# Softmax scores and the first mixture's front product on eight 64x32 tiles of TensorE, with a new load order

## The chip, the cores and the metric

One core of a Trainium2 chip runs the whole program. The metric is the device time of one execution in microseconds, the median of several runs. The profile is taken on one further execution of the same program.

## What is computed

Four batches of eight heads, 576 tokens, 64 numbers a head. 32 packed rows `p` attend to `k` and `v`; the tokens `q` then attend to the 32 packed results. What comes out (2304 tokens of 512 numbers) goes through a layer with `h * cos(h)` and through a mixture of four experts. All is float32; the weights of the first layer arrive as float64.

```
p_packed = softmax(p k^T / 8) v              # 32 rows a head
attn     = softmax(q p_packed^T / 8) p_packed
h = attn @ w_in ; g = h * cos(h) ; x = g @ w_out      # 512 -> 2048 -> 512
out = sum over e of p[:, e] * (relu(x @ w1[e]) @ w2[e])   # 512 -> 1024 -> 512
```

## The kernel before

The program has three parts that flow into each other.

**Attention.** A unit is four of the 32 (batch, head) pairs, so there are eight units; units 2b and 2b+1 make batch b. `attn_p` makes a unit's scores of the packed rows (line `f_s1`, L339), the row maxima (L344), the exponentials (L354), their transposes (L360, copied by L364), the product with `v` (L375), and from it, scaled and masked, the transposed packed rows `ptf` (L380, L386, L390). `attn_q` makes the scores of the tokens (L419), transposes them on VectorE (L425) and does the softmax: maxima, subtraction on GpSimd (L434), exponential (L438), sums, multiplication on GpSimd (L450), transposition (L454), and a split into a rounded part and a remainder (L459, L463), together called `at`. The products L339 and L419 are in plain float32; each holds two heads in 128 rows, with zeros where the heads would mix, and gives 64 columns, so that two of them fill the array.

**First layer, "MoE1".** The 2048 hidden columns go in four groups G of 512. The first product is folded: `m_front` (L508) multiplies the packed rows by `w_in`, once for each G and batch, 16 times in all; `a_front` multiplies the result by `at` (three products each, L193 to L195, for rounded part and remainder), and does the cosine; `a_back` multiplies by `w_out`. `w_block` decodes float64 weights into float32: Abs and a scaling on ScalarE (L249, L270), clamp, shift and sign on VectorE (L256, L260, L265), an addition on GpSimd (L278), and for `w_out` also the split (L274 on ScalarE, L281 on GpSimd). Blocks of `w_in` in group 0 are decoded in halves.

**Second layer, "MoE2".** `b_pair` and `b_back`, the last two thirds of the time, which the change doesn't edit.

The order of the instructions on each engine is fixed when the program is built. Each step is an operation of a planner (`Plan`) with an engine, a duration, the operations that it needs and the buffers that it takes; `Plan.run` goes through time and picks on each engine the ready operation with the lowest key. TensorE and the loads have keys from a table written by hand (`KEYS`). An operation with `alt` may go from GpSimd to VectorE. Loads all stand in one queue, SP's. The raw float64 blocks share two buffers (`raw64`), so the third block waits until GpSimd has finished with the first. Where TensorE has a planned gap in the first 31 us, products of the identity (L966) fill it.

Of the kernel before, what the change touches and what calls it, by code (L numbers as in the profile page):

```python
# [25 lines left out]
class Plan:  # L26
# [32 lines left out]
    def run(self):  # L59
# [14 lines left out]
        while done < len(self.ops):  # L74
# [3 lines left out]
            for eng, l in todo.items():  # L78
                cand = []
                for o in l + ([o for o in todo["POOL"] if o["alt"]] if eng == "DVE" else []):  # L80
                    t = max(o["at"], free.get(eng, 0.0), port if o["port"] else 0.0)
                    ok = True
                    if eng == "PE" and o["key"] > pe[0][0] + self.AHEAD:
                        ok = False
                    for s in o["take"]:
                        if not ends[s["tag"]] or self.bufs[s["tag"]] > 0 and s["no"] != taken[s["tag"]]:
                            ok = False
                            break
                        t = max(t, min(ends[s["tag"]]) + 0.07)
                    if ok:  # L90
                        cand.append((t, o))
                if not cand:
                    continue
                t0 = min(t for t, _ in cand)

                cost = lambda o: 8 * (o["table"] not in (None, table)) if eng == "ACT" else 15 * (o["eng"] != eng)
                t, _, _, o = min((t, o["key"] + cost(o), o["n"], o)
                                 for t, o in [(max(t, t0), o) for t, o in cand if t <= t0 + 0.05])
                if best is None or (t, o["n"]) < best[:2]:
                    best = (t, o["n"], o, eng)  # L100
# [34 lines left out]
def tile_packed_attention_moe_moe2(ctx: ExitStack, tc: tile.TileContext, qT, kT, vk, pT, w_in, w_out, dp, w1, w2, out):  # L135
# [71 lines left out]
    mask = cst.tile([P, P], F32, name="mask")  # L207
    nc.vector.memset(mask, 0.0)
    for i in range(4):
        nc.vector.memset(mask[32 * i:32 * i + 32, 64 * (i % 2):64 * (i % 2) + 64], 1.0)  # L210

    pl = Plan({"pa": -4, "t": -5, "g": 8, "m": 2, "at": 2, "raw64": 2, "wd": 4, "T": 2, "w": 4, "yh": 8, "pz": -2,
               "raw": 4, "s": 4, "aop": 8, "w2": 8, "ys": 5, "pt": -6, "g2": 13, "oacc": NTT,
               **{"B" + x: 1 for x in ("b11", "t1", "t2", "t3", "t4", "b21", "b22")}})
    MB = 1 / 0.27

    def dma(us, f, after=(), take=(), use=(), key=None):
        return pl.op("SP", us, f, after, take, use, key)
# [6 lines left out]
    def w_block(what, G, k, key, pieces=1, ld_key=None):  # L225
# [7 lines left out]
        def f_load():  # L233
            s["raw"] = t = dec.tile([P, 2, 512, 2], U32, tag="raw64", name="raw64", bufs=2)
            load(t.rearrange("p c a b -> p c (a b)"), rows(src.bitcast(U32), r0, slice(2 * c0, 2 * (c0 + cn))))

        ld = dma(1.05 * MB, f_load, take=[sraw], key=key if ld_key is None else ld_key)
        s["ready"] = []
        head = G < HEAD_G
        for p in range(pieces):  # L240
# [31 lines left out]
            def f_hi(c=c):  # L272
                s["w"] = wo.tile([P, 2, 2, 512], F32R, tag="w", name="w", bufs=4)
                nc.scalar.activation(s["w"][:, :, 0], s["D"].bitcast(F32), AF.Copy)  # L274
# [5 lines left out]
            def f_lo(c=c):  # L280
                nc.gpsimd.tensor_tensor(out=s["w"][:, :, 1], in0=s["D"].bitcast(F32), in1=s["w"][:, :, 0].bitcast(F32),  # L281
                                        op=ALU.subtract)


            a = pl.op(*("ACT", 1.15 * r) if head else ("DVE", 0.72 * r), f_and, [ld], [sd] if p == 0 else [], [sraw, sd],
                      key, port=not head)
            a = pl.op("DVE", 0.72 * r, f_clamp, [a], [], [sd], key, port=True)
# [4 lines left out]
            h = pl.op("ACT", 1.1, f_hi, [a], [sw], [sd], key) if what == "out" else None  # L292
            a = pl.op("POOL", 2.45 * r, f_add, [a, l, h], [], [sraw, sd], key)
            if what == "out":
                a = pl.op("POOL", 2.45, f_lo, [a], [], [sw, sd], key)
# [5 lines left out]
    pbd = cst.tile([P, 2, 4, 2, 64], F32, name="pbd")  # L301
    un, ptfs, ats, at_d = {}, {}, {}, {}
    ld_p = dma(2.5 + 0.52 * MB, lambda: load(pbd, pT), key=-2000)

    def load_kv(n, vtag, key):
# [11 lines left out]
        s["ld_v"] = dma(0.59 * MB, f_v, take=[s["v"]], key=key + 0.1)  # L317
# [10 lines left out]
    def attn_p(n, keys):  # L328

        s = un[n]  # L330
        pb = pbd[:, n // 4, n % 4]
        p1, p2, p3, p4 = (pl.slot("pa") for _ in range(4))
        ta, tT, tz = pl.slot("t"), pl.slot("T"), pl.slot("pz")
# [8 lines left out]
        def f_mx():  # L342
            s["mx"] = mx = small.tile([P, 1], F32, tag="mx", name="mx")
            nc.vector.tensor_reduce(out=mx, in_=s["s1"][:, :, :S2], op=ALU.max, axis=AX.XY)  # L344

        def f_nb():
            mx = s["mx"]
            s["nb"] = nb = small.tile([P, 1], F32, tag="nb", name="nb")
            nc.vector.tensor_scalar(out=nb, in0=mx, scalar1=-SCALE, scalar2=None, op0=ALU.mult)
# [679 lines left out]
```

## Time and profile before

| | |
|---|---|
| runs | 1169.66 us median of 3 (1167.9 to 1172.15) |
| profiled execution | span 1170.3 us from first to last instruction; no time outside the span is listed |
| TensorE busy in the span | 1138.4 us (97%) |
| VectorE, ScalarE, GpSimd busy | 752.7, 526.3, 410.2 us |
| mean granted clock of TensorE | 0.991 |

TensorE's share is that of the whole span. The table says nothing about when the other 32 us lie, or which work of the 1138.4 us the change touches; the views by stretch and by line do.

### The profile page before, as it was taken

How to read it: one execution, taken by the hardware profiler on the slowest of the kernel's cores; microseconds unless marked ns; L12 is line 12 of the kernel's file. 1: busy time of each engine (PE TensorE's matmuls, PEld its weight loads, DVE VectorE, ACT ScalarE, POOL GpSimd, SP SyncE). 2: the span in 40 equal slices, each digit the busy share in tenths (PEclk: the TensorE clock that was granted, in tenths of full speed). 3: DMA queues.
4: the chain of work that ended last, by engine and by line, in shares of the span. 5: the costliest groups of instructions: out<-in, count | busy, mean ns of one | idle time of the engine just before them, and what ended most of it. 6: DMA issues, size and time to landing. Idle time of an engine off the chain costs nothing.

```text
span 1170.3 us, 17323 instructions
## 1 busy us (share of the span) xinstructions
PE 1138.4 (97%) x6816; PEld 1023.6 (87%) x6816; DVE 752.7 (64%) x1179; ACT 526.3 (45%) x889; POOL 410.2 (35%) x286
## 2 busy tenths in 40 slices
PE   6599999999999999999999999999999999999998
PEld 5468889989899988998998899989988999899897
DVE  4686867744445777666667666666666666666653
ACT  3778866655555653333334433333335433333320
POOL 1665754443222554122223722222224522222210
PEclk9799999999999999999999999999999999999999
DMA  9854442411215433122224332222231412222101
GB/s 285 285 188 163 169 150 96 153 42 41 82 41 173 134 113 108 58 69 55 72 73 126 108 90 73 72 73 73 72 108 46 136 57 70 55 71 73 54 1 54
DMA packets 54160, 115.96 MB, mean 99 GB/s; under 512 B 5824, under 2 KB 18112, under 8 KB 52032
## 3 DMA queue, kind: packets, MB, share of 16 engines
q1 hardware_dynamic: 54080, 114.87, 30.4%
q8 instruction: 53, 0.87, 0.3%
q14 instruction: 27, 0.22, 0.1%
HBM read 100.70 MB, written 14.16 MB: 98 GB/s over the span
## 4 chain that ended last, share of the span: by engine, by line
PE 91%; DVE 3%; DMA 3%; ACT 2%; POOL 1%; issue 1%; SPq 0%; DVEq 0%; ACTq 0%
PE pa L193 29%; PE pa L195 29%; PE pa L194 29%; PE pa L508 3%; DMA kt<-kT 3%; PE pa L339 1%; PE pa L419 0%; POOL w L628 0%; DVE bop L628 0%; DVE dt L265 0%; PE pa L375 0%; ACT t L539 0%; DVE dt L256 0%; DVE t L542 0%; POOL dt L278 0%
## 5 line engine op out<-in xcount | busy, mean ns | idle before, releaser
L193 PE MATMUL pa<-bop,aop 128*128 128x384 f32 x672 | 226.5, 337 | 3.4 <-DVE p L771 1.4
L194 PE MATMUL pa<-bop,aop 128*128 128x384 f32 x672 | 225.7, 336 | 0.0
L195 PE MATMUL pa<-bop,aop 128*128 128x384 f32 x672 | 225.6, 336 | 0.0
L193 PE MATMUL pa<-w,g 128*128 128x512 f32 x576 | 224.9, 390 | 0.0
L194 PE MATMUL pa<-w,g 128*128 128x512 f32 x576 | 224.7, 390 | 0.0
L195 PE MATMUL pa<-w,g 128*128 128x512 f32 x576 | 224.7, 390 | 0.0
L840 DVE SCALAR_TENSOR_TENSOR oacc<-pa,pr,oacc 128x512 f32<-128x512 f32 x126 | 94.2, 750 | 137.1 <-PE pa L195 137.1
L628 POOL TENSOR_TENSOR aop<-s,aop 128x512 fp32r<-128x512 f32 x33 | 44.8, 1357 | 352.1 <-ACT aop L637 352.1
L193 PE MATMUL pa<-g,w 128*128 128x288 f32 x512 | 153.0, 299 | 0.1
L194 PE MATMUL pa<-g,w 128*128 128x288 f32 x512 | 151.4, 296 | 0.0
L195 PE MATMUL pa<-g,w 128*128 128x288 f32 x512 | 150.9, 295 | 0.0
L559 POOL TENSOR_TENSOR g<-t,g 128x576 fp32r<-128x576 f32 x64 | 93.7, 1478 | 150.5 <-ACT g L556 143.7
L193 PEld LDWEIGHTS pa<-bop,aop 128*128 128x128 f32 x672 | 126.1, 188 | 12.8 <-DVE g L783 3.5
L628 POOL TENSOR_TENSOR w<-raw,w 128x512 fp32r<-128x512 f32 x91 | 120.3, 1343 | 40.6 <-ACT w L637 33.1
L194 PEld LDWEIGHTS pa<-bop,aop 128*128 128x128 f32 x672 | 126.1, 188 | 4.4
L195 PEld LDWEIGHTS pa<-w,g 128*128 128x128 f32 x576 | 108.1, 188 | 23.3
L195 PEld LDWEIGHTS pa<-bop,aop 128*128 128x128 f32 x672 | 126.1, 188 | 0.0
L194 PEld LDWEIGHTS pa<-w,g 128*128 128x128 f32 x576 | 108.2, 188 | 17.8
L193 PEld LDWEIGHTS pa<-w,g 128*128 128x128 f32 x576 | 108.1, 188 | 17.8
L780 ACT ACTIVATE g<-pa 128x384 fp32r<-128x384 f32 x144 | 70.6, 491 | 114.5 <-DVE pa L771 111.5
L780 ACT ACTIVATE g<-p 128x384 fp32r<-128x384 f32 x48 | 25.2, 525 | 172.0 <-DVE p L771 172.0
L193 PEld LDWEIGHTS pa<-g,w 128*128 128x128 f32 x512 | 96.5, 188 | 5.1 <-issue 4.6
(105 smaller groups left out, 2010.7 us busy)
## 6 DMA issues: line engine op xcount, KB each, us to landing
raw<-w SPq DMA_DIRECT2D x96, 512.0 KB, 3.7
at<-at SPq DMA_DIRECT2D x16, 1152.0 KB, 5.2
raw<-w_in SPq DMA_DIRECT2D x8, 1024.0 KB, 6.5
raw<-w_out SPq DMA_DIRECT2D x8, 1024.0 KB, 5.0
kt<-kT SPq DMA_DIRECT2D x8, 576.0 KB, 6.6
vt<-vk SPq DMA_DIRECT2D x8, 576.0 KB, 9.3
qt<-qT SPq DMA_DIRECT2D x8, 576.0 KB, 11.0
y<-yacc SPq DMA_DIRECT2D x24, 192.0 KB, 2.2
```

The lines of the kernel that those rows point to most:

```text
L193: nc.tensor.matmul(o, lhsT=l(0), rhs=r(0), start=first, stop=False, skip_group_check=True)
L194: nc.tensor.matmul(o, lhsT=l(0), rhs=r(1), start=False, stop=False, skip_group_check=True)
L195: nc.tensor.matmul(o, lhsT=l(1), rhs=r(0), start=False, stop=last, skip_group_check=True)
L339: nc.tensor.matmul(s1[64 * a:64 * a + 64, c, :S2], lhsT=pb[:, a, :], rhs=s["kt"][:, a, c * S2:(c + 1) * S2], start=True, stop=True)
L508: nc.tensor.matmul(o[64 * a:64 * a + 64, g], lhsT=ptfs[2 * bb + g][:, 64 * a:64 * a + 64], rhs=w[g]["D"].bitcast(F32)[:, a ^ (bb % 2)], st ...
L559: nc.gpsimd.tensor_tensor(out=s["g"][:, 1], in0=s["t"], in1=s["g"][:, 0].bitcast(F32), op=ALU.subtract)
L628: (nc.vector if on_vector else nc.gpsimd).tensor_tensor(out=dst[:, 1], in0=src, in1=dst[:, 0].bitcast(F32), op=ALU.subtract)
L780: nc.scalar.activation(g["t"][:, 0], s[src], AF.Relu)
L840: nc.vector.scalar_tensor_tensor(out=oa["t"], in0=ot, scalar=sc, in1=oa["t"], op0=ALU.mult, op1=ALU.add)
```

## The change

The two score products and `m_front` now hold one head in 64 rows and give 32 columns: eight such tiles fill the array, two halves of the rows (e) by four quarters of the columns (q). The packed rows lose their zeros (`ptile` for `pbd`, half the bytes), and the mask is gone. A batch is now one unit: its two score products are one step each, with two results, one for each e, and the softmax behind them runs once for each e as it ran for each unit; one transpose L426 and one copy L430 serve a batch. `w_out` of group 0 is decoded in halves as well, and every load of a block in halves is two loads. Subtraction, multiplication and remainder of the token softmax may go to VectorE. The small load of expert shares and its four VectorE steps (`probs`) move from the start to planned time 60. Loads and steps of the first part have keys of their own, one for each batch.

```diff
+    def half_heads(o, l, r, N):
+        for q, e in HQ:            # (0,0) (0,1) (1,0) ... (3,1)
+            nc.tensor.matmul(o(e)[32 * q:32 * q + 32, :N], lhsT=l[64 * e:64 * e + 64, 32 * q:32 * q + 32],
+                             rhs=r(q // 2, q % 2)[64 * e:64 * e + 64], start=True, stop=True)
...
         def f_s1():
-            s["s1"] = s1 = psum2()
-            for a in range(2):
-                for c in range(2):
-                    nc.tensor.matmul(s1[64 * a:64 * a + 64, c, :S2], lhsT=pb[:, a, :],
-                                     rhs=s["kt"][:, a, c * S2:(c + 1) * S2], start=True, stop=True)
+            s["s1"] = [psum2(), psum2()]
+            for c in range(2):
+                half_heads(lambda e: s["s1"][e][:, c], ptile[:, bb].rearrange("p q r -> p (q r)"),
+                           lambda g, a: u[g]["kt"][:, a, c * S2:(c + 1) * S2], S2)
...
+                half_heads(lambda e: s["s2"][e][:, c], ptfs[bb], lambda g, a: u[g]["qt"][:, a, c * S2:(c + 1) * S2], S2)
...
         def f_mm():
             s["o"] = o = psum2()
-            for g in range(2):
-                for a in range(2):
-                    nc.tensor.matmul(o[64 * a:64 * a + 64, g], lhsT=ptfs[2 * bb + g][:, 64 * a:64 * a + 64],
-                                     rhs=w[g]["D"].bitcast(F32)[:, a ^ (bb % 2)], start=True, stop=True)
+            half_heads(lambda e: o[:, e], ptfs[bb], lambda g, a: w[g]["D"].bitcast(F32)[:, a], 512)
...
+            a = pl.op("POOL", 1.16, f_sub, [a], [], [tx], alt=0.78)
...
+            a = pl.op("POOL", 1.16, f_mul, [a], [], [tx], alt=0.78)
...
+            a = pl.op("POOL", 1.42, f_lo, [a], [], [ta, so], alt=0.78)
...
-    w_block("out", 0, 0, KEYS["out0"], ld_key=-400), w_block("out", 0, 1, KEYS["out0"] + 10, ld_key=-390)
+    w_block("out", 0, 0, KEYS["out0"][0], 2, KEYS["load"]["out"])
+    w_block("out", 0, 1, KEYS["out0"][1], 2, KEYS["load"]["out"] + 1)
...
-    probs()
...
+    plan.append((PROBS, len(plan), probs))
```

What this does to the order is seen at three places. In SP's queue, the loads behind the first four, before (`kt`, `vt`, `qt` are the keys, values and tokens of a unit, `raw64` a block of float64 weights):

```order
L185 DMA raw64_214<-w_in 128x2x1024
L185 DMA raw64_266<-w_in 128x2x1024
L185 DMA kt_288<-kT 128x1152
L185 DMA vt_311<-vk 96x1536
L185 DMA kt_324<-kT 128x1152
L185 DMA vt_336<-vk 96x1536
L185 DMA qt_343<-qT 128x1152
L185 DMA qt_356<-qT 128x1152
L185 DMA raw64_367<-w_out 128x2x1024
L185 DMA raw64_408<-w_out 128x2x1024
```

The same place in the changed kernel:

```order
L190 DMA raw64_185<-w_in 128x1024 x2
L190 DMA raw64_255<-w_in 128x1024 x2
L190 DMA kt_291<-kT 128x1152
L190 DMA kt_302<-kT 128x1152
L190 DMA qt_314<-qT 128x1152
L190 DMA raw64_324<-w_out 128x1024 x2
L190 DMA qt_335<-qT 128x1152
L190 DMA raw64_372<-w_out 128x1024 x2
L190 DMA vt_391<-vk 96x1536
```

Both keys of the second batch now come first, the two values behind the two blocks of `w_out`.

On VectorE, where the second block of `w_in` is finished, before (L344 is the maximum over the scores of a unit, L265 the last VectorE step of a half block):

```order
L344 TENSOR_REDUCE mx<-pa 128x1
L260 TENSOR_SCALAR wd<-wd 128x512
L256 TENSOR_SCALAR wd<-wd 128x512
L265 SCALAR_TENSOR_TENSOR wd<-raw_266,wd 128x512
L260 TENSOR_SCALAR wd<-wd 128x512
L442 TENSOR_REDUCE z_352<-x 128x18
L344 TENSOR_REDUCE mx<-pa 128x1
L265 SCALAR_TENSOR_TENSOR wd<-raw_266,wd 128x512
L349 TENSOR_SCALAR nb<-mx 128x1 x2
```

The same place in the changed kernel (L274 is the old L265, L371 the old L344, L483, L467 and L656 are the multiplication, subtraction and remainder that stood on GpSimd):

```order
L274 SCALAR_TENSOR_TENSOR wd<-raw_255,wd 128x512
L483 TENSOR_TENSOR x<-x,z_322 128x576
L488 STREAM_TRANSPOSE xt<-x 128x576
L467 TENSOR_TENSOR x<-x,m_316 128x576
L656 TENSOR_TENSOR at<-xt,at 128x576
L265 TENSOR_SCALAR dt<-dt 128x512
L475 TENSOR_REDUCE z_376<-x 128x18
L269 TENSOR_SCALAR dt<-dt 128x512
L479 TENSOR_SCALAR z_376<-z_376 128x18
L480 RECIPROCAL z_376<-z_376 128x18
L544 TENSOR_TENSOR m<-pa,m 128x2x512
L371 TENSOR_REDUCE mx<-pa 128x1
```

The maxima of the second batch, which need its keys, now stand behind the last step of the block, no longer ahead of it.

On TensorE, from the scores of the second batch to the first `a_front`, before (L339 scores, L508 the front product, L360 and L375 transposes and product with `v`, L193 the first product of `a_front`):

```order
L966 MATMUL pa<-ident 128x128 x12
L339 MATMUL pa<-kt,pbd 64x288 x8
L508 MATMUL pa<-wd,ptf 64x512 x4
L360 MATMUL pa<-ident,a 96x128 x12
L375 MATMUL pa<-vt,aT 32x64 x48
L386 MATMUL pa<-ident,pz 128x128
L193 MATMUL pa<-at,m 128x288
```

The same place in the changed kernel (L347 is `half_heads`, L386 the transposes, L198 the first product of `a_front`):

```order
L347 MATMUL pa<-qt,ptf 32x288 x16
L347 MATMUL pa<-wd,ptf 32x512 x8
L347 MATMUL pa<-kt,ptile 32x288 x16
L386 MATMUL pa<-ident,a 96x128 x6
L198 MATMUL pa<-at,m 128x288
```

The front product now stands ahead of the second batch's scores, and the products with `v` behind the first `a_front`; the filling products are gone here.

## Rows read from the trace of the kernel before

**Rows 1.** The page: TensorE's busy tenths and granted clock in 40 equal slices.

```profile
PE   6599999999999999999999999999999999999998
...
PEclk9799999999999999999999999999999999999999
```

**Rows 2.** Stretches: ends, length, busy us by engine, PEclk, DMA share, GB/s.

```profile
0.00:64.40 64.40, 42.66 (x420) 29.87 (x420) 34.86 (x74) 33.90 (x53) 29.10 (x24) 0.87 0.91 291
64.40:150.00 85.60, 83.40 (x744) 71.19 (x744) 68.37 (x114) 67.46 (x98) 55.74 (x37) 0.98 0.46 161
150.00:414.90 264.90, 264.90 (x1912) 248.27 (x1909) 159.06 (x202) 154.66 (x226) 107.08 (x65) 1.00 0.31 103
414.90:1170.30 755.40, 747.45 (x3746) 674.26 (x3744) 490.45 (x791) 270.32 (x513) 218.31 (x161) 1.00 0.24 74
```

The engines stand in the order TensorE, its weight loads, VectorE, ScalarE, GpSimd.

**Rows 3.** Groups by shape: count, busy us, mean ns, idle before.

```profile
L508 PE MATMUL pa<-wd,ptf 128*64 128x512 f32 x128 | 34.1, 638 | 0.8 <-POOL wd L278 0.8
L339 PE MATMUL pa<-kt,pbd 128*64 128x288 f32 x64 | 10.6, 453 | 10.2 <-DMA kt<-kT 10.2
```

**Rows 4.** The chain that ended last: front products, start and length.

```profile
60.04 3.41 PE pa L508 x8
...
100.99 1.72 PE pa L508 x8
...
361.91 1.87 PE pa L508 x8
```

**Rows 5.** Timeline of TensorE around one front product, and its line's view.

```profile
149.35 0.29 PE L195 MATMUL pa<-g,w 128*128 128x288 f32 x1
149.57 1.94 PE L508 MATMUL pa<-wd,ptf 128*64 128x512 f32 x8
...
151.68 0.29 PE L194 MATMUL pa<-at,m 128*128 128x288 f32 x1
...
L508 PE MATMUL pa<-wd,ptf x8: 592/592/643, 149.6 to 150.9; 128*64 128x512 f32 x8
```

**Rows 6.** Timeline of TensorE around the scores of one unit.

```profile
97.31 0.29 PE L194 MATMUL pa<-g,w 128*128 128x288 f32 x1
97.44 0.29 PE L195 MATMUL pa<-g,w 128*128 128x288 f32 x1
97.67 1.20 PE L339 MATMUL pa<-kt,pbd 128*64 128x288 f32 x8
...
99.03 0.29 PE L194 MATMUL pa<-g,w 128*128 128x288 f32 x1
```

**Rows 7.** Timeline of TensorE: the product with `v`, 32 columns each.

```profile
106.89 0.88 PE L375 MATMUL pa<-vt,aT 96*32 96x64 f32 x48 [0.29 <-ACT aT L364]
107.70 0.33 PE L386 MATMUL pa<-ident,pz 128*128 128x128 f32 x1
```

**Rows 8.** Timeline of several engines on the way to the first `a_front`.

```profile
33.41 2.20 PE L339 MATMUL pa<-kt,pbd 128*64 128x288 f32 x8 [4.76 <-DMA kt<-kT]
...
35.65 0.76 DVE L344 TENSOR_REDUCE mx<-pa 128x1 f32<-128x576 f32 x1 [3.52 <-PE pa L339]
...
36.32 0.68 DVE L265 SCALAR_TENSOR_TENSOR wd<-raw,wd 128x512 uint32<-128x512 uint32 x1
...
37.15 1.29 POOL L278 TENSOR_TENSOR wd<-raw,wd 128x512 uint32<-128x512 uint32 x1 [4.54 <-DVE nb L349]
...
38.49 1.07 PE L508 MATMUL pa<-wd,ptf 128*64 128x512 f32 x2 [0.84 <-POOL wd L278]
...
43.53 0.38 PE L193 MATMUL pa<-at,m 128*128 128x288 f32 x1
```

**Rows 9.** Two stretches of the head, columns as in rows 2.

```profile
30.00:40.00 10.00, 5.74 (x21) 2.41 (x22) 5.60 (x14) 2.58 (x6) 4.20 (x4) 0.69 0.77 242
40.00:64.40 24.40, 16.67 (x180) 11.68 (x177) 15.94 (x26) 21.14 (x30) 19.22 (x11) 0.79 0.92 321
```

**Rows 10.** ScalarE's groups before 64.4 us: Abs of half and whole blocks.

```profile
L249 ACT ACTIVATE wd<-raw 128x512 f32<-128x512 f32 x4 | 2.7, 670 | 0.7 <-DMA raw<-w_in 0.7
L249 ACT ACTIVATE dt<-raw 128x1024 f32<-128x1024 f32 x2 | 2.3, 1168 | 0.0
```

More of the change, by code (lines that the diff above doesn't have):

```diff
@@ L77, in run @@
                 pe.pop(0)
[L78 to L86, printed above, removed]
-                            ok = False
[L88 to L100, printed above, removed]
@@ new lines, in run @@
+            for ahead in (self.AHEAD, 1e9):
+                if best is not None:
+                    break
+                for eng, l in todo.items():
+                    cand = []
+                    for o in l + ([o for o in todo["POOL"] if o["alt"]] if eng == "DVE" else []):
+                        t = max(o["at"], free.get(eng, 0.0), port if o["port"] else 0.0)
+                        ok = True
+                        if eng == "PE" and o["key"] > pe[0][0] + ahead:
+                            ok = False
+                        need = {}
+                        for s in o["take"]:
+                            k = need[s["tag"]] = need.get(s["tag"], 0) + 1
+                            if len(ends[s["tag"]]) < k or self.bufs[s["tag"]] > 0 and s["no"] != taken[s["tag"]] + k - 1:
+                                ok = False
+                                break
+                            t = max(t, sorted(ends[s["tag"]])[k - 1] + 0.07)
+                        if ok:
+                            cand.append((t, o))
+                    if not cand:
+                        continue
+                    t0 = min(t for t, _ in cand)
+                    cost = lambda o: 8 * (o["table"] not in (None, table)) if eng == "ACT" else 15 * (o["eng"] != eng)
+                    t, _, _, o = min((t, o["key"] + cost(o), o["n"], o)
+                                     for t, o in [(max(t, t0), o) for t, o in cand if t <= t0 + 0.05])
+                    if best is None or (t, o["n"]) < best[:2]:
+                        best = (t, o["n"], o, eng)
@@ L231, in w_block, with f_load @@
         wblk[what, G, k] = s
[L233 to L237, printed above, removed]
+        def f_load(p=0):
+            if p == 0:
+                s["raw"] = dec.tile([P, 2, 512, 2], U32, tag="raw64", name="raw64", bufs=2)
+            t, n = s["raw"], 2 // pieces
+            load(t[:, p * n:(p + 1) * n].rearrange("p c a b -> p c (a b)"),
+                 rows(src.bitcast(U32), r0 + p * P, slice(2 * c0, 2 * (c0 + cn)), n))
+        key_l = key if ld_key is None else ld_key
+        lds = []
+        for p in range(pieces):
+            lds.append(dma(1.05 * MB / pieces, lambda p=p: f_load(p), take=[] if p else [sraw], use=[sraw] if p else [],
+                           key=key_l, begun=lds[-1:]))
         s["ready"] = []
         head = G < HEAD_G
+        prev, his = [], []
         for p in range(pieces):
```

370 lines of the change are left out of this document (202 added, 168 removed), and 3 rows, old and new, of the table KEYS.

## The prediction

> **What bounds the kernel now.** I read the page's slices first. TensorE is busy nine tenths or more in all of the 40 slices but the first two and the last, and its clock falls only in the first ones [rows 1]. So time can come from two places: less work on TensorE where it never stops, or an earlier end of the head, where it waits. The stretches cut the span at three points: the first `a_back` product (64.4 us), the end of the attention work (150) and the first product of MoE2 (414.9). From 150 to 414.9 TensorE is busy 264.90 of 264.90 us while VectorE and ScalarE work under 61% of it: every microsecond taken from TensorE there is a microsecond of the kernel. From 64.4 to 150 it is still busy 83.40 of 85.60, but VectorE (68.37) and ScalarE (67.46) work 80% and 79%. Before 64.4 it is busy 42.66, filling products included, at a mean clock of 0.87 of 2.4 GHz, and the DMA engines are 91% busy. The last stretch holds 747.45 busy of 755.40 and nothing that the change edits [rows 2]. The groups by shape size the work that changes: 128 instructions L508, and 64 L339 that waited 10.2 us for keys [rows 3].
>
> **The front product, 16 times.** Between the ordinary products at 149.35 and 151.68 lie 2.33 us; two of them at their spacing of 0.13 leave 2.06 for the front product. Its eight instructions (four float32 products of two passes each) take 592 ns at the median, 4.7 us together inside 1.94: they overlap by twos, in four rounds whose first and last start 1.3 us apart, so 0.43 a round [rows 5]. That is two cycles a column at the full clock (512 x 2 / 2.4 GHz). Four rounds are 1.71, the rest, 0.35, is the change of tile shape and the run-out. The new product has 16 instructions for eight tiles. If all eight run at once, that is two rounds: 0.86 less. For eight more starts I allow 0.06, under half of what the product with `v` spends on eight of its 48 instructions, everything included (0.81 us from 106.89 to 107.70, 17 ns each) [rows 7]. So **2.06 becomes 1.26: 0.80 less** (bounds 0.72 and 0.86 while the tiles overlap). The trace shows four tiles side by side: 48 instructions of 64 columns in 0.81 are twelve rounds of 0.053 and 0.17 around them [rows 7]. No row shows two halves of the rows at once. The opposite bound is therefore that e = 0 and e = 1 take turns, a rival below.
>
> A rule speaks against the change. The row first: 24 products with `v` of two passes each would need 24 x 0.053 = 1.28 us if the second pass of one held back the first pass of the next tile; they take 0.81 [rows 7]. The Trainium skill (TensorE: Matmul & The Clock Gate, Part 3, on what overlaps) says that matmuls start and end strictly in program order. Were the two passes of each product neighbours in that order, eight tiles would be a staircase of 8 x 0.43 + 0.35 = 3.8 us instead of 1.26. The trace disagrees with that reading for four tiles, and I take the row.
>
> **The scores, four and four.** By the same reckoning one unit's L339 costs 1.59 us from 97.44 to 99.03 less two spacings of 0.13, 1.33, again four rounds, of 0.24 for 288 columns [rows 6]. A batch has 32 instructions in four rounds of eight, so it costs what one unit cost, plus 0.10 for starts: 1.43 instead of 2.66, **1.23 less** (bounds 0.9 and 1.33). L419 has the same shape. One transpose of the packed result for two saves 0.3 a batch [rows 7].
>
> **Where this counts.** (a) 150 to 414.9: eleven front products, 21.2 us apart from 149.6 to 361.91 [rows 4, 5], **8.8 us**, all of it on the path, since no other engine is near its limit. (b) 64.4 to 150: three front products (2.4), scores of batches 2 and 3 (four steps, 4.9) and two transposes (0.6): 7.9. Taking all of it would leave 77.7 us for VectorE's 68.4 and ScalarE's 67.5, 88% and 87%, in chains that go back and forth between engines. TensorE already idles 2.2 us there at 80%. Bounds 0 and 7.9; I take half, **4 us**. The two front products before 64.4 count to the head.
>
> **The head.** Today the last half block of `w_in` is late because of order. The scores of the fourth unit wait for keys until 33.41, the maximum L344 stands ahead of the sign step L265 on VectorE and waits 3.52 us with it, GpSimd waits 4.54 for that, and the front product ends at 39.56, the first `a_front` starts at 43.53 [rows 8]. In the new order the sign step stands ahead of the maximum, so up to 3.5 us go. The keys come ahead of values and tokens, so the second batch's scores find them. But the second batch's first six transposes now stand ahead of the first `a_front`. With the front product done at 39.56 - 3.5 = 36 they follow scores (1.43) and a maximum for each half (0.76 [rows 8]), then an exponential and the transposes themselves, about as long again each: some 40 at the earliest, and VectorE has the remainder of the front product and three new steps to do in between. Of the 3.5 us I give the first `a_front` 1. Between there and the first `a_back` ScalarE bounds: 21.14 busy of 24.40 from 40 us on, while from 30 to 40 it had 2.58 of 10 [rows 9]. With both `w_out` blocks ahead of the second batch's values, and half as many bytes of packed rows, some of its 4.7 us of decoding (two Abs and two scalings of 1.17) moves into that idle time; halves cost it 0.67 twice for 1.17 once, four pairs of Abs and scaling, 0.7 us, and about as much more for the rounded part [rows 10]. Net **2 us** for the head (bounds -2 and +5). Cover for the rest: the subtraction, multiplication and remainder that go to VectorE use the 4.4 us that it idles from 30 to 40 [rows 9]; if that cover is gone they cost 0.8 us each, three times, the duration of the nearest VectorE step of that width, L344. `probs` moves from an idle VectorE into the head's end: four steps under 0.3 us each. Its load stands behind a `w_in` block that waits for GpSimd to free a raw buffer; if it lands late, VectorE waits, and two steps of the cosine queue behind. At 291 GB/s [rows 2] a block of 1.05 MB is 3.6 us, the price of one such collision. No fillers stand between 24 us and the first `a_front`, so those products may run at the lower clock of 1.2 GHz; today the clock is 0.69 and 0.79 of full there too [rows 9], so I take no difference, within the bounds.
>
> **The sum.** 8.8 + 4 + 2 = 14.8 us from the profiled 1170.3: 1155.5. MoE2 keeps its 755.4. The profiled span lies 0.6 above the median of the runs, 1169.66, so the forecast for the median is **1155 us**.
>
> **Rivals.**
> 1. *The other engines take all of the second stretch.* For: both at 80% there. Against: they keep TensorE at 97% now. Then (b) is 0, and if `probs` collides as well the head gains nothing: 1169.7 - 8.8 = 1161, to 1164 with the collision.
> 2. *The head opens up.* If ScalarE's decoding moves fully into the idle time, the head gives 5 and (b) 7: 1169.7 - 8.8 - 12 = 1149.
> 3. *The tiles bring nothing:* four rounds as before, because only the column quarters overlap and the hardware sorts them well. Then the two score steps of a batch and the front product cost what they did and only the head is left: 1168.
> 4. *Slower: the two row halves take turns in the written order.* A column's e = 1 starts when its e = 0 has run both passes (0.86 us), and the next column's e = 0 with it: five turns, 5 x 0.86 + 0.35 = 4.6 us a front product, 2.6 more than now. Fourteen on the path cost 36 us, the four score steps 5.2 for 2.66 each, 10 us: about 1213. It decides from about 2.1 us a front product on. For it: no row shows row halves side by side. Against: weights, moving rows and results of the halves lie on different partitions or in different banks (`o[:, 0]`, `o[:, 1]`), and columns show no such wait [rows 7]. The Trainium skill (same page, Part 3, measured speedups) gives 10.6 times for sixteen tiles over rows and columns, which agrees with 1.26; no run here shows it yet.
>
> **How the numbers follow.** The forecast and its neighbourhood, 1150 to 1160.5, get 0.60, rival 1 0.17, rival 2 0.13, rival 3 0.04, rival 4 0.06. From 1149 to 1164 lie the forecast, most of rival 1 and half of rival 2: about 0.81. A measurement of this kernel can tell about 0.3%, 3.5 us, from no change. Faster by more than that: forecast, rivals 1 and 2, 0.89; within it, rival 3 and a little of rival 1, 0.05; slower 0.06.
>
> **What would show it.** Front products: 16 instructions that all start within half a microsecond, about 1.25 us between ordinary products. First `a_back` near 62 us, first MoE2 product near 400, MoE2 again 755 long. Stretch (b) should show TensorE idle of about 6 us in place of 2.2, with ScalarE or VectorE named as what ended it. I am wrong if front products keep 2 us or more, or if the first `a_back` comes after 66.

## The result, and the profile after

The changed kernel takes 1156.07 us at the median of 4 runs (1154.18 to 1159.73), the kernel before 1169.98 in the same set (4 runs, 1167.9 to 1172.15): a ratio of 0.9886, 95% interval 0.9859 to 0.9913. The profiled execution of the changed kernel took 1154.18 us with a span of 1152.4; the one of before 1172.15 with 1170.3. In both the time is the span plus some 1.8 us.

The page, as in [rows 1]: TensorE's busy tenths and granted clock. The second row shows that the clock of the first slices is lower than before ([rows 1]), not higher.

```profile
PE   7698999999999999999999999999999999999998
...
PEclk8699999999999999999999999999999999999999
```

The stretches, cut at the first `a_back` product, at the first of the last eleven front products and at the first product of MoE2; columns as in [rows 2].

```profile
0.00:60.50 60.50, 41.58 (x481) 28.51 (x481) 36.52 (x76) 34.55 (x58) 22.79 (x23) 0.80 0.83 270
60.50:143.00 82.50, 76.91 (x834) 67.97 (x827) 66.72 (x116) 64.01 (x93) 46.69 (x33) 0.98 0.51 180
143.00:399.40 256.40, 256.30 (x2001) 245.19 (x2001) 158.79 (x204) 157.07 (x226) 118.98 (x71) 1.00 0.32 110
399.40:1152.40 753.00, 746.78 (x3746) 674.30 (x3744) 488.49 (x789) 270.84 (x514) 221.04 (x163) 1.00 0.24 75
```

The groups by shape, as in [rows 3]: twice the instructions, 11 us less of TensorE for the front products, and no wait of TensorE for keys ahead of the scores (10.2 us before).

```profile
L347 PE MATMUL pa<-wd,ptf 64*32 64x512 f32 x256 | 23.1, 622 | 6.4 <-POOL wd L288 5.7 <-ACT ptf L430 0.6
L347 PE MATMUL pa<-kt,ptile 64*32 64x288 f32 x128 | 8.1, 478 | 0.0
```

The same cut of the kernel before (first `a_back` at 64.44, the front product of 149.57 [rows 5], the first MoE2 product at 414.95) gives this comparison:

| stretch | before | after | gained | forecast |
|---|---|---|---|---|
| head, to the first `a_back` | 64.4 | 60.5 | 3.9 | 2 |
| middle, to the front product of 149.57 / 143.00 | 85.1 | 82.5 | 2.6 | 4 |
| full, to MoE2 | 265.4 | 256.4 | 9.0 | 8.8 |
| MoE2 | 755.4 | 753.0 | 2.4 | 0 |
| span | 1170.3 | 1152.4 | 17.9 | 14.8 |

The profiled execution of after is the shortest of its four and that of before the longest, so these two traces lie 17.9 us apart and the medians 13.9. Where executions of one program differ is shown below: in the head.

A front product, TensorE's timeline, to set against [rows 5]. From the last ordinary product before it to the second one behind it are 1.48 us, where they were 2.33.

```profile
142.77 0.29 PE L200 MATMUL pa<-g,w 128*128 128x288 f32 x1
143.00 1.09 PE L347 MATMUL pa<-wd,ptf 64*32 64x512 f32 x16
144.01 0.40 PE L198 MATMUL pa<-at,m 128*128 128x288 f32 x1
144.25 0.30 PE L199 MATMUL pa<-at,m 128*128 128x288 f32 x1
```

All 16 instructions start within half a microsecond (line view: count, shortest, median and longest in ns, first and last start).

```profile
L347 PE MATMUL pa<-wd,ptf x16: 588/601/614, 143.0 to 143.5; 64*32 64x512 f32 x16
```

The chain that ended last has eleven front products, first and last of them here, 20.42 us apart; they were 21.23 apart in [rows 4, 5]. Nine of the ten steps are 20.38 and one is 20.74, so the usual step is 0.85 shorter.

```profile
143.07 1.02 PE pa L347 x16
...
347.23 1.02 PE pa L347 x16
```

The scores of a whole batch, 32 instructions, now stand where those of one unit stood in [rows 6]: 1.59 us from the last product before to the second behind, less two spacings of 0.13: 1.33, for two units instead of one.

```profile
64.54 0.29 PE L200 MATMUL pa<-g,w 128*128 128x288 f32 x1
64.76 1.20 PE L347 MATMUL pa<-kt,ptile 64*32 64x288 f32 x32
65.89 0.40 PE L198 MATMUL pa<-g,w 128*128 128x288 f32 x1
66.13 0.29 PE L199 MATMUL pa<-g,w 128*128 128x288 f32 x1
```

The way to the first `a_front`, several engines, to set against [rows 8]. The first weights land in time for an Abs (L258, L249 before) at 16.01; it began at 21.14 before. None of these rows waits for keys. The front product's last pieces start at 30.34 and 31.20 (38.49 before). Behind them VectorE makes `m` (L544) and only then the maximum (L371); TensorE's transposes L386 stand ahead of `a_front` and wait 3.25 us for the exponential.

```profile
16.01 0.69 ACT L258 ACTIVATE wd<-raw 128x512 f32<-128x512 f32 x1 [1.22 <-DMA raw<-w_in]
...
30.34 1.07 PE L347 MATMUL pa<-wd,ptf 64*32 64x512 f32 x2 [1.11 <-POOL wd L288]
...
31.20 1.06 PE L347 MATMUL pa<-wd,ptf 64*32 64x512 f32 x2
...
33.37 1.22 DVE L544 TENSOR_TENSOR m<-pa,m 128x1024 fp32r<-128x1024 f32 x1
...
34.51 0.75 DVE L371 TENSOR_REDUCE mx<-pa 128x1 f32<-128x576 f32 x1
...
36.56 0.72 ACT L380 ACTIVATE a<-pa,nb 128x576 f32<-128x576 f32 x1
...
37.43 1.52 PE L386 MATMUL pa<-ident,a 128*96 128x128 f32 x6 [3.25 <-ACT a L380]
38.60 0.59 PE L198 MATMUL pa<-at,m 128*128 128x288 f32 x1
```

Two stretches of the head, as [rows 9]: ScalarE works 9.07 us of the ten from 30 to 40 (2.58 before) and 15.27 of the 20.5 behind (21.14 of 24.40 before). The clock is 0.50 of full from 30 to 40, that is 1.2 GHz throughout; in the ten microseconds before, TensorE had been busy for 4.88.

```profile
20.00:30.00 10.00, 4.88 (x12) 0.51 (x12) 9.90 (x21) 2.97 (x6) 5.55 (x5) 0.64 0.81 303
30.00:40.00 10.00, 6.41 (x48) 4.11 (x49) 9.88 (x20) 9.07 (x17) 2.96 (x3) 0.50 0.87 246
40.00:60.50 20.50, 14.48 (x196) 11.46 (x195) 11.80 (x23) 15.27 (x25) 12.62 (x10) 0.84 0.72 221
```

TensorE's waits from 60.5 to 143: who waited for whom, us in total, times, longest. These are the five largest. None is long, and all three other engines are named.

```profile
PE pa L199 <- POOL g L587: 1.4, 2, 1.1
PE pa L426 <- DVE pz L410: 0.8, 1, 0.8
PE pa L198 <- DVE m L544: 0.8, 1, 0.8
PE pa L198 <- DVE t L580: 0.5, 2, 0.4
PE pa L403 <- ACT at L493: 0.5, 1, 0.5
```

### The profile page after: what moved, and what is told of

It reads as the page before. It is cut to its first block, busy times and chain, and to the rows that moved or that the text cites. A ratio compares the mean times of both kernels' runs of the same rounds, so it can differ in the third digit from the quotient of the medians.

```text
span 1152.4 us, 17770 instructions
## 1 busy us (share of the span) xinstructions
PE 1121.6 (97%) x7050; PEld 1016.0 (88%) x7050; DVE 750.5 (65%) x1182; ACT 526.5 (46%) x889; POOL 409.5 (36%) x288
## 4 chain that ended last, share of the span: by engine, by line
PE 90%; DVE 4%; ACT 2%; DMA 1%; issue 1%; POOL 1%; SPq 0%; DVEq 0%; ACTq 0%
PE pa L198 30%; PE pa L199 29%; PE pa L200 29%; PE pa L347 1%; DMA raw<-w_in 1%; POOL wd L288 1%; PE pa L403 0%; DVE wd L265 0%; DVE bop L656 0%; DVE wd L274 0%; DVE wd L269 0%; PE pa L386 0%; SPq L190 0%; ACT t L567 0%; DVE m L544 0%
## 5 line engine op out<-in xcount | busy, mean ns | idle before, releaser
L198 PE MATMUL pa<-bop,aop 128*128 128x384 f32 x672 | 226.5, 337 | 1.9 <-DVE p L799 1.4
L198 PE MATMUL pa<-w,g 128*128 128x512 f32 x576 | 225.0, 391 | 0.0
L656 POOL TENSOR_TENSOR aop<-s,aop 128x512 fp32r<-128x512 f32 x36 | 49.4, 1374 | 349.1 <-ACT aop L665 344.9
L198 PE MATMUL pa<-g,w 128*128 128x288 f32 x512 | 153.1, 299 | 1.7 <-DVE m L544 0.8
L656 POOL TENSOR_TENSOR w<-raw,w 128x512 fp32r<-128x512 f32 x93 | 121.9, 1332 | 40.6 <-ACT w L665 33.0
L198 PEld LDWEIGHTS pa<-bop,aop 128*128 128x128 f32 x672 | 126.1, 188 | 10.7 <-DVE g L811 2.9
L198 PEld LDWEIGHTS pa<-w,g 128*128 128x128 f32 x576 | 108.1, 188 | 17.8
L198 PEld LDWEIGHTS pa<-g,w 128*128 128x128 f32 x512 | 96.6, 189 | 4.2 <-DVE t L580 1.4
```

The lines of the kernel that those rows point to most:

```text
L198: nc.tensor.matmul(o, lhsT=l(0), rhs=r(0), start=first, stop=False, skip_group_check=True)
L656: (nc.vector if on_vector else nc.gpsimd).tensor_tensor(out=dst[:, 1], in0=src, in1=dst[:, 0].bitcast(F32), op=ALU.subtract)
```

## The experiments

They ran in three sets, on three chips, on which the kernel before took 1168.57, 1169.46 and 1171.22 us at the median (19, 11 and 23 runs). So times are compared by their ratio to before in the same set (0.001 is 1.2 us), and the stages by one profile each; the row "after" is from the set of the result. "Weights" is the start of the first Abs on the first weights.

| kernel | median us | ratio, interval | weights | first `a_front` | first `a_back` | middle | full | MoE2 |
|---|---|---|---|---|---|---|---|---|
| before | | 1 | 21.1 | 43.5 | 64.4 | 85.1 | 265.4 | 755.4 |
| after | 1156.07 | 0.9886, 0.9859 to 0.9913 | 16.0 | 38.6 | 60.5 | 82.5 | 256.4 | 753.0 |
| e1 full rows | 1172.14 | 1.0031, 1.0014 to 1.0047 | 17.4 | 40.9 | 63.0 | 86.8 | 265.6 | 753.0 |
| e2 double front | 1169.62 | 1.0009, 0.9991 to 1.0026 | 18.0 | 42.5 | 64.1 | 86.8 | 266.0 | 752.8 |
| e3 fillers | 1158.04 | 0.9906, 0.9875 to 0.9937 | 16.2 | 37.8 | 61.2 | 82.4 | 256.4 | 752.8 |
| e4 no Abs | 1156.72 | 0.9900, 0.9871 to 0.9929 | 20.2 | 43.1 | 64.8 | 83.0 | 256.1 | 752.8 |
| e5 whole loads | 1158.84 | 0.9908, 0.9885 to 0.9931 | 17.3 | 39.0 | 60.7 | 82.5 | 256.4 | 753.4 |
| e6 extra load | 1159.57 | 0.9921, 0.9901 to 0.9942 | 22.8 | 44.1 | 66.2 | 83.6 | 256.4 | 753.3 |
| e7 w_in sooner | 1159.14 | 0.9921, 0.9901 to 0.9941 | 16.3 | 41.9 | 65.2 | 82.0 | 256.4 | 753.1 |
| e8 row order | 1157.52 | 0.9906, 0.9886 to 0.9926 | 18.5 | 41.9 | 63.4 | 82.5 | 256.4 | 753.0 |
| e9 old loads | 1159.63 | 0.9901, 0.9877 to 0.9924 | 18.1 | 44.3 | 66.2 | 83.4 | 256.4 | 753.4 |
| e10 w_out whole | 1168.65 | 0.9982, 0.9966 to 0.9999 | 15.9 | 37.9 | 61.1 | 87.7 | 256.1 | 762.4 |
| e11 no choice of engine | 1164.37 | 0.9949, 0.9924 to 0.9974 | 17.6 | 40.1 | 61.9 | 91.1 | 256.1 | 753.0 |
| e12 no maximum | 1155.06 | 0.9864, 0.9842 to 0.9886 | 17.6 | 39.7 | 61.8 | 83.4 | 256.4 | 752.8 |

**e1, the rows of the tiles undone.** Tiles of 128 rows whose other half holds zeros, four at a time in two turns, in the same program.

```
+    for e in range(2):
+        for x in [ptiles[e]] + [pfull[b][e] for b in range(B)]:
+            nc.vector.memset(x[64 * (1 - e):64 * (1 - e) + 64], 0.0)
...
-    HQ = [(q, e) for q in range(4) for e in range(2)]
+    HQ = [(q, e) for e in range(2) for q in range(4)]
...
-            nc.tensor.matmul(o(e)[32 * q:32 * q + 32, :N], lhsT=l[64 * e:64 * e + 64, 32 * q:32 * q + 32],
-                             rhs=r(q // 2, q % 2)[64 * e:64 * e + 64], start=True, stop=True)
+            nc.tensor.matmul(o(e)[32 * q:32 * q + 32, :N], lhsT=l[e][:, 32 * q:32 * q + 32],
+                             rhs=r(q // 2, q % 2), start=True, stop=True)
```

> The changed kernel with its order and loads kept, but each of the eight tiles is 128 rows high, the other half filled with zeros in the packed operand, so that only four column quarters can run side by side, in two turns: four rounds in place of two. Theory (the gain is TensorE time, counted one to one from 143 us on and about half before): a front product between ordinary ones costs about 2.05 us in place of 1.25, the stretch of eleven front products is 8.8 us longer, the stretch before it 3 to 5 us, the head 0 to 2; whole 12 to 15 us more than the changed kernel, within 3 us of the kernel before. Rival (the gain is the new order and the loads): under 4 us more than the changed kernel.

The whole gain is gone: 1.0031 of before, with the new order of steps and loads in place; against the changed kernel that is 17 us, where 12 to 15 were expected. A front product is back where it was in [rows 5], 2.05 us (2.32 from the last product before to the second behind, less two spacings), and the full stretch is 265.6 us long, 265.4 before. TensorE's timeline:

```profile
149.57 0.29 PE L200 MATMUL pa<-g,w 128*128 128x288 f32 x1
149.80 1.92 PE L351 MATMUL pa<-wd,ptf 128*32 128x512 f32 x16
151.65 0.40 PE L198 MATMUL pa<-at,m 128*128 128x288 f32 x1
151.89 0.29 PE L199 MATMUL pa<-at,m 128*128 128x288 f32 x1
```

So the tiles carry the change. The rest of it, orders and halves, brings nothing by itself; the interval, 1.0014 to 1.0047, says rather a small loss. Part of that may be e1's own: it adds ten memsets on VectorE at the start and a second copy of the packed result for each batch. Its middle stretch has the same order as the changed kernel's; columns as in [rows 2]:

```profile
63.02:149.80 86.78, 82.17 (x831) 69.46 (x827) 66.81 (x116) 64.39 (x94) 46.13 (x32) 0.98 0.47 169
```

It is 4.3 us longer than in the changed kernel and 1.7 longer than in the kernel before.

**e2, the front product done twice.** It measures what one costs in each stretch.

```
-            half_heads(lambda e: o[:, e], ptfs[bb], ...)
+            for _ in range(2):
+                half_heads(lambda e: o[:, e], ptfs[bb], ...)
```

> The changed kernel with every front product issued twice, the second time over the first (same result). Each second one is two more rounds of 0.43 us. Theory: 16 x 0.86 = 13.8 us more work on TensorE, of which the eleven in the full stretch cost 9.5 to 10, the three before it half of 2.6, the two in the head 0 to 2: 11 to 13 us more than the changed kernel. Rival (VectorE and ScalarE bound the full stretch too): under 6 us more.

```profile
150.88 1.95 PE L347 MATMUL pa<-wd,ptf 64*32 64x512 f32 x32
```

32 instructions take 1.95 us in TensorE's timeline where 16 took 1.09: two more rounds are 0.86, and the step between front products grows from 20.42 to 21.28. The eleven of the full stretch cost 9.5 us, one to one. The three of the middle stretch are 2.6 us of work and lengthened it by 4.3, at a clock of 0.96 in place of 0.98; TensorE's idle time there stayed, 5.7 us for 5.6. So work added in a fixed order counted whole here too. By the ratios e2 is 14 us above the changed kernel, for an expected 11 to 13. Stretches:

```profile
64.08:150.88 86.80, 81.14 (x882) 69.25 (x875) 67.02 (x116) 63.54 (x93) 46.67 (x33) 0.96 0.48 170
```

**e3, products of the identity in the gaps up to 62 us, not 31.**

```
-        if b["start"] < 31 and b["start"] - a["end"] > 1:
+        if b["start"] < 62 and b["start"] - a["end"] > 1:
```

> The changed kernel, with the filling products also in TensorE's planned gaps up to 62 us (63 more products of the identity), so that TensorE has work between 24 and 42 us. Theory (the granted clock of 0.50 from 30 to 40 us costs the head a little): clock 1.00 there, first a_front 1 to 2 us sooner, whole 0 to 2 us less than the changed kernel. Rival (the fillers stand in the way of what becomes ready early): 1 to 3 us more.

The mean clock rose from 0.988 to 0.996, from 30 to 40 us to 1.00, and nothing was gained: 0.9906. The first `a_front` came 21.6 us after the weights (22.6 in the changed kernel), the first `a_back` 23.5 behind it (21.9). The low clock of the head costs nothing that shows. Whether the fillers took back behind `a_front` what the clock gave ahead of it, this run doesn't separate.

**e4, ScalarE relieved.** The Abs inside the cosine is left out.

```
-            nc.scalar.activation(s["t"], s["t"], AF.Abs)
+            pass
```

> The changed kernel without the absolute value before the sine on ScalarE (64 steps of 0.675 us, 12 of them between the first a_back product and 143 us), so the cosine is not the reference's. Theory (that stretch is held by ScalarE and VectorE at about 80%): TensorE's idle time in it falls from 5.6 us to 2 to 4, the whole is 2 to 4 us less than the changed kernel. Rival (it is held by single chains through the fixed order, not by an engine's load): under 1.5 us less.

ScalarE's work in the middle stretch falls from 64.0 to 55.9 us, the stretch stays (83.0 for 82.5). But the granted clock fell as well, from 0.98 to 0.95, and TensorE was busy 1.2 us longer with the same products. A fairer neighbour is e6 below, whose steps in this stretch are those of the changed kernel and whose clock there is 0.95 too: 83.6 us, 5.2 of them idle. Against it e4 is 0.7 us shorter, with 4.8 idle. So ScalarE's 8 us less were worth under 1 us; its load doesn't hold the stretch. Stretches, columns as in [rows 2], of e4:

```profile
64.77:147.72 82.95, 78.14 (x833) 68.82 (x826) 66.00 (x115) 55.91 (x79) 46.71 (x32) 0.95 0.50 176
```

And of e6:

```profile
66.19:149.80 83.61, 78.42 (x831) 69.11 (x826) 65.97 (x115) 62.98 (x91) 45.79 (x32) 0.95 0.49 175
```

**e5, whole loads of the first blocks, decoded in halves.**

```
+            if p:
+                return
-            t, n = s["raw"], 2 // pieces
+            t, n = s["raw"], 2
```

> The changed kernel with each of the first four weight blocks brought by one load of 1.05 MB instead of two of 0.52 MB; they are still decoded in halves, and no engine's instructions change place. Theory (the first weights' landing sets the head: what the head gained came from fewer bytes ahead of the first usable weights): the first Abs begins about 1.8 us later than in the changed kernel (0.52 MB at about 0.29 MB per us), the first a_front and all after it shift by as much, about 1157.9 us, ratio to before 0.990. Rival (the new order of the decode steps set the head): the order is the same, so 1156.1 us and ratio 0.989.

Undecided. The weights came 1.3 us later in this profile and the first `a_front` 0.4; the runs differ among themselves (1154.76 to 1160.56) by more than the theories do.

**e6, 1.18 MB more ahead of the first weights.**

```
+    spare = cst.tile([P, 2, 2, S], F32, name="spare")
...
+                if (what, G, k) == ("in", 0, 0):
+                    for i in range(2):
+                        load(spare[:, i], kT[i // 2, i % 2])
```

> The changed kernel with two more loads of 0.59 MB, which nothing uses, in SP's queue just ahead of the first w_in loads; no other instruction moves. Theory (landing sets the head, one to one): the first Abs begins about 4 us later (1.18 MB at about 0.29 MB per us), the first a_front too, and the whole kernel ends about 4 us later, near 1160 us, ratio 0.992. Rival (the order of the decode steps, or PE's own work before them, sets the head, and the loads have slack): under 1 us, about 1156.5 us.

ScalarE's timeline: it waits 5.03 us for the weights.

```profile
22.75 0.66 ACT L261 ACTIVATE wd<-raw 128x512 f32<-128x512 f32 x1 [5.03 <-DMA raw<-w_in]
```

The first `a_front` follows 21.3 us later, at 44.1, and the ratio is 0.0035 above that of the changed kernel, 4 us, as expected. The runs alone don't show it: the intervals of the two ratios overlap, and in its own set e6 lies only 2.0 us above e8. The profiles tell more. In after, e3, e5, e12, e8, e4 and e6, whose steps stand in one order, the first Abs begins at 16.0, 16.2, 17.3, 17.6, 18.5, 20.2 and 22.8, and the spans are 1152.4, 1152.8, 1153.0, 1154.4, 1155.4, 1156.6 and 1159.6: the end follows the landing nearly one to one.

**e7, the first weights ahead of one block of values.**

```
-            'load': {'in': -1715.6,
+            'load': {'in': -1985.0,
```

> The changed kernel with the load key of the first w_in blocks at -1985 in place of -1715.6, so that they stand ahead of one vt load of 0.59 MB in SP's queue; the planner lays the rest out anew, and the first front product comes before the second scores. Theory (landing sets the head): the weights land 2 us sooner, the first a_front too, about 1154 us, ratio 0.987, better than both kernels. Rival (the first softmax, which now waits longer for its v, then holds the front product instead, or the new order loses in the middle stretch what the head gains): 1156 us or more.

The rival. ScalarE begins on the weights at 16.31 and no longer waits for them, against 16.01 in the changed kernel's profile, so no 2 us were won there; but the values came later, and now the packed rows `ptf` are what the front product waits for. TensorE's timeline:

```profile
26.92 2.36 PE L347 MATMUL pa<-wd,ptf 64*32 64x512 f32 x16 [0.46 <-ACT ptf L430]
```

**e8, the tiles issued by row half.**

```
-    HQ = [(q, e) for q in range(4) for e in range(2)]
+    HQ = [(q, e) for e in range(2) for q in range(4)]
```

> The changed kernel with its eight tiles issued by row half: the four column groups of the upper 64 rows, then the four of the lower, in place of upper and lower in turn. Theory (tiles of both row halves and all four column groups are in the array at once, whatever the order they come in): a front product still takes about 1.25 us between ordinary products and the step between front products stays 20.4 us, 1156 us. Rival (tiles start strictly in order and a row half holds the next one up, so only the alternation makes the overlap): a front product goes back to about 2.05 us, the step to 21.2 us, about 1169 us.

The step stays 20.42 and the front product 1.09, in TensorE's timeline:

```profile
145.70 0.29 PE L200 MATMUL pa<-g,w 128*128 128x288 f32 x1
145.92 1.09 PE L347 MATMUL pa<-wd,ptf 64*32 64x512 f32 x16
146.94 0.40 PE L198 MATMUL pa<-at,m 128*128 128x288 f32 x1
147.18 0.30 PE L199 MATMUL pa<-at,m 128*128 128x288 f32 x1
```

The order of the tiles is of no account: both row halves are in the array at once either way. Against e1, which has this order too, it is the 64 rows that make it so.

**e9, the old order of loads under the new order of steps.**

```
     order = pl.run()
+    for n in range(4):
+        un[n]["ld_v"]["start"] = un[n]["ld_k"]["start"] + 0.01
+    un[3]["ld_q"]["start"] = un[2]["ld_q"]["start"] + 0.01
```

> The changed kernel with its first sixteen loads in the order that the kernel before has (each unit's values right behind its keys, all of q2 and q3 ahead of w_out); the bytes ahead of the first weights are the same, and no engine's instructions change place. Theory A (what counts in the head is the arrival of the first weights, and behind them that of the second batch's keys): the weights land as in the changed kernel, the second batch's keys k2 and k3 come behind one more load of 0.59 MB, about 2 us later; in the changed kernel the scores of the second batch stand behind the front product, which ends at 32 us, so 0 to 2 us are lost: 1156 to 1158 us. Rival (the order of the loads is what brought the head its 4 us): the first a_front goes back to about 43 us and the kernel to about 1160 us.

The first `a_front`, at 44.3, and the time are about those that the rival gave, and 26.3 us lie between weights and `a_front`, where the changed kernel, e3 to e6, e8 and e12 have 21.3 to 23.4. (The ratio alone doesn't tell it from the changed kernel.) But the keys are not what is late, as theory A had it: `w_out` now comes behind values and tokens, ScalarE waits for it, and in its order the exponential of the second softmax (L471) and the rounding of `m` (L541, at 37.64) stand behind; in the changed kernel they begin at 31.14 and 32.31. ScalarE's timeline:

```profile
36.50 0.66 ACT L258 ACTIVATE dt<-raw 128x512 f32<-128x512 f32 x1 [2.95 <-DMA raw<-w_out]
37.07 0.67 ACT L471 ACTIVATE x<-x 128x576 f32<-128x576 f32 x1
37.64 1.01 ACT L541 ACTIVATE m<-pa 128x1024 fp32r<-128x1024 f32 x1
```

**e10, the first `w_out` blocks whole.**

```
-    w_block("out", 0, 0, KEYS["out0"][0], 2, KEYS["load"]["out"])
+    w_block("out", 0, 0, KEYS["out0"][0], 1, KEYS["load"]["out"])
```

(and the second block likewise)

> The changed kernel with the first two w_out blocks loaded and decoded whole, as before; the planner lays the steps around them out anew. Prediction's reckoning (halves cost ScalarE about 1.4 us and let GpSimd and ScalarE begin sooner): the first a_back comes 0 to 1.5 us later or sooner, 1155 to 1158 us. Rival (the halves of w_out are what brought the first a_back forward): the stretch from the first a_front to the first a_back grows by over 2 us, 1159 us or more.

The head did as reckoned: the first `a_back` comes 0.6 us later, and from the first `a_front` to it are 23.3 us for 21.9. The time is 1168.65 all the same: the middle stretch is 5.2 us longer and MoE2 9.5, so the rival is right in its number and not in its reason. In MoE2's first 51 us TensorE is busy 44.98 at a clock of 0.93; in the changed kernel 50.54 at 1.00. Stretches:

```profile
404.00:455.00 51.00, 44.98 (x219) 41.23 (x218) 36.25 (x51) 20.04 (x38) 22.26 (x16) 0.93 0.29 84
```

The edit lies 340 us ahead of that. The planner, with other pieces and durations to place, laid out all engines anew, and a first step of ScalarE in MoE2 (L821) now waited 7.2 us, by the view of waits for the store of `y`. So this run prices a layout, not the halves.

**e11, no choice between GpSimd and VectorE.**

```
-            a = pl.op("POOL", 1.16, f_sub, [a], [], [tx], alt=0.78)
+            a = pl.op("POOL", 1.16, f_sub, [a], [], [tx])
```

(and the multiplication and the remainder likewise)

> The changed kernel with the second softmax's subtraction, multiplication and remainder on GpSimd alone, as before, in place of the planner's choice between GpSimd and VectorE; the planner lays the rest out anew. Theory (the middle stretch is held by chains from engine to engine, not by one engine's load, and the moved steps are few): 1156 to 1158 us. Rival (the moved steps are what keeps the middle stretch at 82.5 us): it grows by 2 us or more, 1158 us or more.

Again the layout: the middle stretch grows by 8.5 us, 5.5 of it one wait of TensorE for a step of ScalarE, while VectorE is busy 65.4 and GpSimd 51.9 of its 91.1. The clock there is 0.93 for 0.98, which is in the 8.5 as well: TensorE is busy 2.2 us longer. TensorE's timeline:

```profile
100.90 0.61 PE L198 MATMUL pa<-g,w 128*128 128x288 f32 x1 [5.50 <-ACT g L584]
```

The rival is right in its number. Whether the moved steps themselves are needed, apart from the order laid around them, this run doesn't separate.

**e12, shorter chains on VectorE and GpSimd.**

```
             def f_m2(e=e, x3=x3):
+                if bb:
+                    return
...
             def f_sub(v=False, e=e, x3=x3):
+                if bb:
+                    return
```

> The changed kernel without the maximum of the second softmax and its subtraction in batches 1 to 3: six reductions of 0.75 us on VectorE and six subtractions of 0.8 to 1.2 us, five of them on GpSimd, all in the stretch between the first a_back and the last eleven front products; every other instruction stands where it stood. The output differs from the reference where the maximum matters for rounding. Theory (chains in a fixed order hold the middle stretch: shorter chains let TensorE idle less): the stretch falls from 82.5 us by 1 to 4 us, TensorE's idle time in it from 5.6 us to 2 to 4.5; 1152 to 1155 us. Rival (the stretch is held by TensorE's own work and by waits elsewhere): under 0.5 us, 1156 us.

The theory fell. With 5.5 us less on VectorE and 6.6 less on GpSimd, the middle stretch is 83.4 us for 82.5, TensorE's idle time in it 5.0 for 5.6. The clock is 0.95 for 0.98 here; against e6 at the same clock the stretch is 0.2 us shorter and the idle time 0.2 less. Stretches:

```profile
61.76:145.16 83.40, 78.41 (x831) 69.29 (x827) 61.26 (x108) 62.81 (x91) 40.13 (x27) 0.95 0.49 176
```

The ratio, 0.9864, is not told apart from that of the changed kernel.

## Why the prediction came out

**The front product** was to fall from 2.06 to 1.26 us, 0.80 less. Read in the same way it fell to 1.21, 0.85 less, and so did nine of the ten steps between front products (0.81 on the mean of all). The argument held in each part: two rounds of 0.43 in place of four (e2 shows 0.86 for two more), and the 0.35 for the change of tile shape stayed. Rival 3 fell with that, and e1 shows the reverse: without half-height tiles the four rounds are back.

**Row halves taking turns (rival 4)** fell too: eight tiles run at once, and e8 shows that the order in which they are issued doesn't matter. The line view gives 16 instructions of about 0.60 us, 9.6 us of them, inside 1.09. The rule that the prediction weighed (the Trainium skill, TensorE: Matmul & The Clock Gate, Part 3, matmuls start and end strictly in program order) would have made 3.8 us of it if the two passes of a float32 product were neighbours in that order; the trace disagrees with that reading, now for both halves of the rows as well as for the columns. In which order the passes are issued no view here shows, so the rule itself is neither refuted nor shown.

**(a), 8.8 us,** measured 9.0, on a stretch where TensorE idles 0.1 us of 256.4. This is the term that the experiments carry best: e1 loses it whole, e2 pays it again.

**The scores** were to cost 1.43 a batch and cost 1.33: 32 starts cost no more than 8.

**(b), 4 us of a possible 7.9,** measured 2.6. The sign that was named is there: TensorE's idle time rose from 2.2 us to 5.6 (6 was forecast), while its work fell by 6.0 (82.9 in the same cut of before, to 76.91). The reason given was the load of ScalarE and VectorE, and that fell: relieving ScalarE (e4) or VectorE and GpSimd (e12) was worth under 1 us at the same clock. So half of 7.9 came near for the wrong reason. e1 splits the 2.6, by one profile each: in the same order the tiles bring 4.3 of the 5.3 us that they take from TensorE's busy time, and the new order by itself costs 1.7. The stretch answers to the layout: e10 and e11, laid out anew, lost 5.2 and 8.5 us there, with VectorE and ScalarE busy for less than 80% of it. The waits are many and short, and which of them hold the 5.6 us stays open. Rival 1 had it right that the others take part of what TensorE gives up, but not by being full.

**The head, 2 us,** measured 3.9 between these two profiles, and its reason failed. The prediction reckoned from the order of steps: 3.5 us less before the front product, most of it lost again to the transposes ahead of `a_front`. That pattern is there, in a smaller size: the last front product starts 15.2 us after the weights (17.4 before), 2.2 less, and the transposes then wait 3.25 us. From weights to `a_front` it comes out even: 22.6 for 22.4. What moved the head between these profiles is when the weights land, 16.0 for 21.1, which the sum left out. The bytes ahead of the first usable weights fell from about 5.1 MB (packed rows 0.52, six loads of 0.59, a block of 1.05) to 4.3 (0.26, the same six, half a block of 0.52): 0.8 MB, an estimated 2.7 us at the 291 GB/s of [rows 2]. The rest is within the scatter: with the same loads ahead the weights came between 16.0 and 20.2 us in the profiles of after, e3, e4, e8 and e12, `a_front` 21.6 to 23.4 us after them, and the first `a_back` at 60.5 to 64.8. Of the kernel before there is one profile, so how much of the 3.9 belongs to the change is not shown. e6 moves the landing on purpose, and the kernel with it. The order of the loads behind them counts too, in the one trace of e9, because `w_out` must be there when ScalarE's steps of it come.

**Between the first `a_front` and the first `a_back`** the prediction had ScalarE as the bound. ScalarE did take its decoding forward, as forecast (9.07 us of work from 30 to 40), and has 5.9 us less behind; still the way took 21.9 us for 20.9. That reason fell too; what holds this way instead was not tried.

**MoE2, 0,** measured 2.4 less. All kernels with the new planner but e10 have 752.8 to 753.4, the one profile of before 755.4. The steps of MoE2 are as they were, but the diff gives the planner other rules of order (a `begun` condition also on a step of `b_back`, and a wider look ahead), and TensorE idles 6.2 us there for 8.0; which rule does it was not tried.

**The sum** of 14.8 stands against 13.9 of the medians and 17.9 of the profiles. The base was read wrongly: 1170.3 is a span, and that execution took 1172.15, 2.5 above the median of 1169.66, not 0.6. Since span and 0.6 were used together, the forecast was in effect the median less the sum, and no harm came of it. Of the terms (a) is off by 0.2, (b) by 1.4, the head by 1.9 and MoE2 by 2.4, in both directions. That the median, 1156.07, lies 1 us from the forecast of 1155 is therefore partly luck: 8.8 of the 14.8 us have their reason shown, the tiles' share of (b) has it in part, and the head came out for another reason.

## What to carry to other kernels

Where a contraction fills half of the rows and a quarter of the columns, eight tiles side by side took 1.21 us where the same eight padded to 128 rows took 2.05 (e1), and two orders of issue gave the same. All of it counted where TensorE never stops. Where engines hand data back and forth, 4.3 of 5.3 us counted in a fixed order, and the new order took 1.7 back. In a program whose order is fixed beforehand, an edit of a few durations can lose more through the new layout, hundreds of microseconds away, than it is worth: compare with the order held fixed. And look at when the first usable bytes land: in the profiles with one order of steps, the end of this kernel followed their landing nearly one to one.

## What was not expected of the hardware

The landing of the first weights scatters by 4 us between profiles with the same loads ahead (16.0 to 20.2), and the spans with it (1152.4 to 1156.6). The runs of the changed kernel scatter by 5.6 us (1154.18 to 1159.73); that the landing is the reason there too is likely but not shown, since only one of them has a trace. A clock of 0.50 from 30 to 40 us cost nothing that shows: raising it to 1.00 with fillers (e3) left the time as it was.
